# Down weights in three loads of four feature tiles, between transposing loads

## The chip, the cores and the metric

One Trainium2 chip, one of its cores, one launch. The metric is the device time of the kernel in microseconds (us). Five engines work beside each other, each with its own queue of instructions that it works off in order: TensorE (PE in the profile, its weight loads PEld), VectorE (DVE), ScalarE (ACT), GpSimd (POOL) and SyncE (SP), which here does nothing but issue transfers. An engine waits for another one, or for a transfer, at a semaphore.

## The reference

A transformer layer in bfloat16 with S = 2048 tokens and D = 640: linear attention with a softmax feature map (32 heads of 20), then a gated bilinear feed-forward with F = 1536.

```python
def _A_ref(x, wqkv, w_phi, wo):                     # H = 32, Dh = 20
    q, k, v = ...                                   # x @ wqkv, split in heads
    pq = jnp.einsum("bhsd,hdf->bhsf", q, w_phi)
    pk = jnp.einsum("bhsd,hdf->bhsf", k, w_phi)
    phi_q = jnp.concatenate([_softmax(pq, axis=-1), _softmax(-pq, axis=-1)], axis=-1)
    phi_k = jnp.concatenate([_softmax(pk, axis=-1), _softmax(-pk, axis=-1)], axis=-1)
    kv = jnp.einsum("bhsf,bhsd->bhfd", phi_k, v)
    z  = jnp.einsum("bhsf->bhf", phi_k)
    num = jnp.einsum("bhqf,bhfd->bhqd", phi_q, kv)
    den = jnp.einsum("bhqf,bhf->bhq", phi_q, z)[..., None] + 1e-6
    return (num / den, heads joined) @ wo

def _B_ref(x, w_gate, w_up, w_down):
    h = (x @ w_gate) * (x @ w_up)
    return jnp.einsum("bsf,fd->bsd", h, w_down)

h = x + _A_ref(_layernorm(x), A_wqkv, A_w_phi, A_wo)
h2 = h + _B_ref(_layernorm(h), B_w_gate, B_w_up, B_w_down)
```

Only w_down, called Wd in the kernel (1536 x 640, twelve feature tiles of 128 rows), is loaded in another way by the change.

## The kernel before

The tokens are cut into 16 tiles of 128, and four tiles make a block. The program is built as a list of operations (Prog.op, line 195), each with an engine, a function that emits it, and the registers (Reg) that it reads (rd), writes (wr) or adds to (app). From the registers follow the semaphores to wait on. Each operation belongs to a unit with a short name, set by U(...). The order on each engine isn't planned: ORDER (lines 74 to 148) writes it out by hand as a list of unit names, and place (line 244) takes each engine's operations in this order, choosing only which buffer of a pool an operation gets, by modelled times.

The units around the change, for a token tile t:

- kt, Kt, vt: keys, their normalisation and the values. The values go to vaug.
- At: products of keys and values (kv_mm), summed over all tiles; the last readers of vaug as values.
- qt: scores of the queries on TensorE, their maximum on VectorE, exponentials on ScalarE into one of three eq buffers. Qt: sum and reciprocal on VectorE, a product on GpSimd (line 999), and two transposing transfers on SP (line 553) that turn eq into phiqT. The eq buffer is free for another tile when both have landed.
- nt: the attention's numerator on TensorE, from phiqT; quotient into ob on VectorE (line 1075); a transposing transfer on SP that turns ob into oT. For the even block oT lies in the buffer named phik, for the odd block behind Wd in the buffer named vaug. Tiles 0 and 1 are turned by TensorE instead.
- ht: product with Wo on TensorE (phik,Wo or vaug,Wo in the profile), residual, statistics, and the normalised row hb, which SP turns into hT.
- fb.ft.j: gate and up products of block b, feature tile ft.
- T0 to T3: sums of blocks of Wd on GpSimd (weight_sums, line 1247), the first readers of Wd. d0, d1: the down products of tiles 0 and 1 on TensorE (down_raw, line 1279), which read Wd directly.

Wd takes the place of the values in memory: it lies in the buffer BV, named vaug in the profile, and may be written when the last At is done; alias (line 236) hands the readers of vaug on to R_Wd. The unit ld (line 1432) loads it in one transfer of 1920 KB, issued by SP. In SP's order it stands between the two transposes of query tile 4:

`Q5 Q5 n2 n3 Q7 Q7 Q4 ld Q4 Q6 n7 n5 Q6 Q8 Q8`

SP's plain loads (load, line 548) take their semaphores in turn from a ring of eight called w, its transposes from a ring of eight called tr. All of SP's transfers run through one queue of the profile (q1).

Of the kernel before, what the change touches and what calls it, by code (L numbers as in the profile page):

```python
# [11 lines left out]
P = 128  # L12
# [135 lines left out]
}  # L148


# [274 lines left out]
def bass_sequential_preLN__linear_kernel_hedgehog__glu_gated_bilinear__prompt_kernel(  # L425
        nc, A_x, A_wqkv, A_w_phi, A_wo, B_x, B_w_gate, B_w_up, B_w_down, out):
    with ExitStack() as ctx:
        _build(ctx, nc, A_x, A_wqkv, A_w_phi, A_wo, B_w_gate, B_w_up, B_w_down, out)
# [5 lines left out]
def _build(ctx, nc, A_x, A_wqkv, A_w_phi, A_wo, B_w_gate, B_w_up, B_w_down, out):  # L434
    g = Prog(nc, ctx)
# [4 lines left out]
    def regs(n):  # L440
        return [Reg() for _ in range(n)]
# [57 lines left out]
    Wd = BV[:, 0:NF * D].rearrange("p (f n) -> p f n", f=NF)  # L499
# [37 lines left out]
    R_Wo, R_Wgu, R_Wd = regs(NC), regs(2), Reg()  # L537
# [7 lines left out]
    R_phiqT = [[regs(4) for _ in range(2)] for _ in range(2)]  # L545
    R_hT, R_oT, R_hhT = [regs(4) for _ in range(2)], [regs(4) for _ in range(2)], [[regs(4) for _ in range(NF)] for _ in range(2)]

    def load(out_, in_, wr, mb, eng="SP", at=0.0):
        return g.op(eng, lambda e: e.dma_start(out_, in_), wr=wr, dma=("w", 8), t=0.5, lat=0.4 if at else 0.6, size=mb / 0.38, at=at)

    def transpose(out_, in_, rd, wr, use=(), t=1.27, size=0.45, lat=0.3, at=0.0):

# [24 lines left out]
    def U(name):  # L577
        g.unit = name
# [3 lines left out]
    def load_wnat(w, cs=(0, NC), eng="SP", at=0.0):  # L582
        c0, c1 = cs
        load(Wnat[:, c0:c1, :], A_wqkv[P * c0:P * c1, D * w:D * (w + 1)].rearrange("(c p) n -> p c n", p=P), R_Wnat[c0:c1],
             0.3 * (c1 - c0), eng=eng, at=at)
# [4 lines left out]
    def load_x(b):  # L590
        load(x_all[:, 4 * b:4 * b + 4, :], A_x[0, 4 * P * b:4 * P * (b + 1), :].rearrange("(t p) n -> p t n", p=P), [R_x[b]], 0.9)

    def load_wv(c0, c1, at):
        load(Wp[:, c0:c1, 2 * D:3 * D], A_wqkv[P * c0:P * c1, 2 * D:3 * D].rearrange("(c p) n -> p c n", p=P), R_Wp[2][c0:c1], 0.16 * (c1 - c0), at=at)
# [36 lines left out]
    for a in range(NC):  # L631
        lo, hi = CH[a]
        n = hi - lo + 1
# [795 lines left out]
    g.alias([r for a in R_phiqT for b_ in a for r in b_], R_Wnat + R_WT[0] + R_WT[1])  # L1429
    g.alias([r for x in R_hhT for y in x for r in y] + [r for x in R_hT for r in x] + R_oT[0], [r for p in R_phik for r in p])  # L1430
    g.alias(R_oT[1] + [R_Wd], R_vaug)
    U("ld")
    load(Wd[:, :, :], B_w_down.rearrange("(f p) n -> p f n", p=P), [R_Wd], 1.92)
    def each(f, b):
        for t in range(4 * b, 4 * b + 4):
            f(t)
# [82 lines left out]
```

## Time and profile before

| | |
|---|---|
| median of 3 runs | 267.46 us (267.43 to 267.47) |
| profiled execution | 267.44 us |
| its span, first to last instruction | 265.7 us |
| granted TensorE clock | 1.0 throughout |
| bytes moved | 28.65 MB, mean 108 GB/s |
| the down weights' load | issued at 93.54 us, 0.59 us on SP, landed 8.2 us after its issue |

The span is 1.7 us shorter than the time of the same execution; what lies around it is start and end. Times within the profile count from the span's start. In a timeline each line is a merged piece: start, duration, engine (SPq is SP's queue), line of the kernel, operation, written tile<-read tiles, and in brackets idle time and what ended it. A transfer has a duration on SP, which is its issue alone, and a time from issue to landing, which the view of one tile gives as minimum, median and maximum. The view of windows gives for each stretch its busy time on each engine with the number of instructions, then the granted clock, the mean busy share of the 16 DMA engines and the GB/s.

### The profile page before, as it was taken

Reading aid. Unit: us, or ns where it says so; the run is one execution under the profiler, and the core shown is the slowest. Engines: PE = TensorE matmul, PEld = TensorE weight load, DVE = VectorE, ACT = ScalarE, POOL = GpSimd, SP = SyncE. Lnnn points to the kernel's source line nnn. Section 1 sums busy time; section 2 is a strip of 40 time slices with the busy share of each in tenths; the row PEclk is TensorE's granted clock in tenths of the full one; section 3 lists DMA queues with packets and bytes.
Section 4 is the critical chain, followed back from the end, with each engine's and each line's share of the span. In section 5 each row is a group of like instructions: output and inputs, shape, how many; then the busy total and the mean of one; then the engine's idle time right before and its main releaser. Section 6 shows DMA issues by size and latency. Waiting matters only on the chain.

```text
span 265.7 us, 6271 instructions
## 1 busy us (share of the span) xinstructions
PE 261.3 (98%) x2439; PEld 200.2 (75%) x2439; DVE 223.0 (84%) x418; ACT 177.6 (67%) x387; POOL 190.4 (72%) x243
## 2 busy tenths in 40 slices
PE   8999999999999999999999999999999999999995
PEld 8877777776877887777766887777777777777774
DVE  1999999999999876998989788987778788676683
ACT  2567999999857998769562695764856555645221
POOL 5446889999932879999974889359856474648652
PEclk9999999999999999999999999999999999999999
DMA  7996989933255489666866414300420501001012
GB/s 188 305 142 140 170 177 397 390 107 73 40 80 100 93 245 211 130 112 134 119 121 128 46 25 79 99 4 0 52 49 14 88 0 52 1 2 51 4 68 78
DMA packets 67678, 28.65 MB, mean 108 GB/s; under 512 B 57920, under 2 KB 66368, under 8 KB 67648
## 3 DMA queue, kind: packets, MB, share of 16 engines
q1 hardware_dynamic: 66432, 27.77, 47.9%
q10 hardware_dynamic: 1216, 0.48, 0.7%
q8 instruction: 19, 0.31, 0.5%
q14 instruction: 11, 0.09, 0.1%
HBM read 11.82 MB, written 2.62 MB: 54 GB/s over the span
## 4 chain that ended last, share of the span: by engine, by line
PE 80%; POOL 13%; DVE 2%; DMA 2%; issue 1%; ACT 1%; SPq 0%; ACTq 0%
PE ps L657 54%; PE ps L1210 25%; POOL phik L950 10%; DMA phiqT<-eq 2%; POOL eq L999 1%; POOL rs L714 1%; PE ps L746 1%; DVE Wp L864 1%; DVE Ssum L947 1%; ACT eq L933 1%; POOL vaug L645 0%; SPq L553 0%; DVE phiqT L806 0%; DVE ps L925 0%; DVE t L702 0%
## 5 line engine op out<-in xcount | busy, mean ns | idle before, releaser
L657 PE MATMUL ps<-Wp,xT 128*128 128x320 bf16 (+1 forms) x606 | 89.1, 299 | 0.0
L657 PEld LDWEIGHTS ps<-Wp,xT 128*128 128x128 bf16 x606 | 58.0, 98 | 22.6 <-ACT phik L933 0.3
L1240 POOL TENSOR_TENSOR phik<-phik,gate 128x512 bf16<-128x512 bf16 x34 | 40.0, 1182 | 25.9 <-DVE phik L1237 25.5
L1220 ACT ACTIVATE eq<-ps 128x256 f32<-128x256 f32 x110 | 37.4, 386 | 23.0 <-PE ps L1210 18.8
L1210 PE MATMUL ps<-phik,Wgu 128*128 128x256 bf16 (+1 forms) x228 | 50.6, 304 | 0.0
L950 POOL TENSOR_TENSOR phik<-phik,Rk 128x1280 bf16<-128x1280 bf16 x16 | 37.4, 2357 | 5.8 <-DVE Rk L949 4.8
L657 PE MATMUL ps<-phik,Wgu 128*128 128x256 bf16 (+1 forms) x260 | 33.3, 281 | 0.0
L657 PEld LDWEIGHTS ps<-phik,Wgu 128*128 128x128 bf16 x260 | 24.9, 98 | 5.8 <-DMA phik<-hb 0.2
L1337 POOL TENSOR_TENSOR phiqT<-phiqT,x_all 128x320 f32<-128x320 f32 x26 | 21.7, 844 | 9.7 <-ACT phiqT L1335 9.6
L925 DVE TENSOR_REDUCE ps<-ps 128x1 f32<-128x640 f32 (+1 forms) x32 | 26.1, 819 | 2.9 <-PE ps L657 2.9
L1210 PEld LDWEIGHTS ps<-phik,Wgu 128*128 128x128 bf16 x228 | 21.9, 98 | 5.7 <-ACT eq L1220 0.2
L657 PE MATMUL ps<-vaug,phik 128*128 128x63 bf16 (+1 forms) x308 | 25.9, 238 | 0.0
L987 DVE TENSOR_REDUCE Sq<-eq 128x66 f32<-128x1320 bf16 x16 | 24.2, 1514 | 1.2 <-ACT eq L933 1.2
L1237 DVE TENSOR_TENSOR phik<-ps,eq 128x512 bf16<-128x512 f32 x28 | 19.2, 687 | 6.3 <-PE ps L1210 6.2
L1335 ACT ACTIVATE phiqT<-ps 128x320 f32<-128x320 f32 x26 | 11.4, 437 | 19.3 <-PE ps L657 19.2
L947 DVE TENSOR_REDUCE Ssum<-phik 128x64 f32<-128x1280 bf16 x16 | 23.4, 1462 | 0.0
L1235 DVE TENSOR_TENSOR gate<-ps,eq 128x512 bf16<-128x512 f32 x27 | 18.5, 686 | 5.2 <-PE ps L1210 2.9
L657 PEld LDWEIGHTS ps<-vaug,phik 128*128 128x128 bf16 x308 | 18.1, 97 | 5.3
L999 POOL TENSOR_TENSOR eq<-eq,rq 128x660 bf16<-128x660 bf16 x16 | 20.9, 1306 | 0.8
L933 ACT ACTIVATE eq<-ps,nb,rs 128x300 bf16<-128x300 f32 (+2 forms) x26 | 17.2, 690 | 6.0 <-DVE nb L928 4.2
L1342 DVE TENSOR_TENSOR outb<-ps,phiqT 128x320 bf16<-128x320 f32 x27 | 12.9, 488 | 6.6 <-PE ps L657 5.1
L1139 ACT ACTIVATE gate<-ps 128x256 bf16<-128x256 f32 (+1 forms) x26 | 10.4, 403 | 10.2 <-PE ps L657 9.6
(169 smaller groups left out, 527.4 us busy)
## 6 DMA issues: line engine op xcount, KB each, us to landing
x_all<-in_A_x_dram SPq DMA_DIRECT2D x4, 640.0 KB, 10.8
out_dram<-outb SPq DMA_DIRECT2D x13, 160.0 KB, 1.8
Wgu<-in_B_w_gate_dram SPq DMA_DIRECT2D x1, 1920.0 KB, 11.1
Wgu<-in_B_w_up_dram SPq DMA_DIRECT2D x1, 1920.0 KB, 16.6
vaug<-in_B_w_down_dram SPq DMA_DIRECT2D x1, 1920.0 KB, 8.2
Wp<-in_A_wqkv_dram SPq DMA_DIRECT2D x1, 800.0 KB, 5.1
phiqT<-in_A_wqkv_dram SPq DMA_DIRECT2D x1, 800.0 KB, 6.3
Wo<-in_A_wo_dram SPq DMA_DIRECT2D x1, 800.0 KB, 6.3
```

The costliest lines, as they stand in the source:

```text
L657: ins = e.matmul(o_, lhsT=l_, rhs=r_, start=s_, stop=p_, skip_group_check=True)
L925: g.op("DVE", lambda e: e.tensor_reduce(out=mx(), in_=src(), axis=AX.XY if len(src().shape) == 3 else AX.X, op=ALU.max, apply_absolute_val ...
L933: g.op("ACT", lambda e, s=s, sc=sc, to=to, of=of: e.activation(out=to(s), in_=of(), func=ACT.Exp, bias=nb[:, i:i + 1], scale=sc[:, t:t + 1 ...
L947: g.op("DVE", lambda e: e.tensor_reduce(out=Ssum[:, vs.i, :], in_=x, axis=AX.X, op=ALU.add), rd=R_phik[t], wr=vs.R, use=[vs], t=1.39, lat=1.5)
L950: g.op("POOL", lambda e: e.tensor_tensor(out=x, in0=x, in1=Rk[:, vr.i, :].unsqueeze(2).to_broadcast([P, 2 * H, DH]), op=ALU.mult), rd=vr.R ...
L987: g.op("DVE", lambda e: e.tensor_reduce(out=Sq[:, vs.i, :].rearrange("p (w g) -> p w g", w=NQ), in_=feat(0, NQ).rearrange("p w (g f) -> p ...
L999: return e.tensor_tensor(out=x, in0=x, in1=rq[:, vr.i, :].rearrange("p (w h) -> p w h", h=HW).unsqueeze(3).to_broadcast([P, NQ, HW, DH]), ...
L1210: ins = e.matmul(o_, lhsT=l_[0](c), rhs=m_, start=fr, stop=False, skip_group_check=True)
L1220: g.op("ACT", lambda e: e.activation(out=half(s[i], 256 * h, 256 * (h + 1)), in_=PS[v.i][:, bk, 256:512], func=ACT.Copy), rd=[v.R[bk]], wr ...
L1237: g.op("DVE", lambda e: e.tensor_tensor(out=hhT[:, hb_, ft, :], in0=PS[v.i][:, 1, :], in1=half(s[1]), op=ALU.add), rd=[v.R[1]] + s[1].R, w ...
L1240: g.op(eng, lambda e: e.tensor_tensor(out=hhT[:, hb_, ft, :], in0=hhT[:, hb_, ft, :], in1=gate[:, vg.i, :], op=ALU.mult), rd=R_out + vg.R, ...
L1337: g.op("POOL", lambda e: e.tensor_tensor(out=slot(x), in0=slot(x), in1=x_all[:, t, c], op=ALU.add), rd=x.R + [R_h[t]], wr=x.R, use=[x], t= ...
```

## The change

The load of Wd is cut into three, one for each four feature tiles (640 KB each), as units ld0, ld1 and ld2. The first writes R_Wd, the other two add to it (app), so that each reader of Wd waits for all three. In SP's order ld0 goes between Q5 and n2, ld1 between n3 and Q7, ld2 between Q7 and Q4. The two transposes of Q4 are now neighbours. Everything else in the orders of all engines is kept.

```diff
     "SP":
-        "Q0 Q1 Q0 Q1 Q2 Q2 Q3 Q3 Q5 Q5 n2 n3 Q7 Q7 Q4 ld Q4 Q6 n7 n5 Q6 Q8 Q8 h3 n4 h2 Q10 Q10 n6 Q14 Q14 Q9 n8 Q9 h5 h7 Q11 Q11 "
...
+        "Q0 Q1 Q0 Q1 Q2 Q2 Q3 Q3 Q5 Q5 ld0 n2 n3 ld1 Q7 Q7 ld2 Q4 Q4 Q6 n7 n5 Q6 Q8 Q8 h3 n4 h2 Q10 Q10 n6 Q14 Q14 Q9 n8 Q9 h5 h7 "
...
-    def load(out_, in_, wr, mb, eng="SP", at=0.0):
-        return g.op(eng, lambda e: e.dma_start(out_, in_), wr=wr, dma=("w", 8), t=0.5, lat=0.4 if at else 0.6, size=mb / 0.38, at=at)
+    def load(out_, in_, wr, mb, eng="SP", at=0.0, first=True):
+        return g.op(eng, lambda e: e.dma_start(out_, in_), **{"wr" if first else "app": wr}, dma=("w", 8), t=0.5, lat=0.4 if at else 0.6, size=mb / 0.38, at=at)
...
-    U("ld")
-    load(Wd[:, :, :], B_w_down.rearrange("(f p) n -> p f n", p=P), [R_Wd], 1.92)
+    for j in range(3):
+        U("ld%d" % j)
+        load(Wd[:, 4 * j:4 * j + 4, :], B_w_down[4 * P * j:4 * P * (j + 1), :].rearrange("(f p) n -> p f n", p=P), [R_Wd], 0.64,
+             first=j == 0)
```

4 rows, old and new, of the table ORDER are left out of this document.

## The prediction

> **What bounds the kernel now.** I read the page first (busy shares, chain that ended last), then the chain in order of time, then the timelines of SP's queue and of TensorE around the edited place.
>
> ```profile
> span 265.7 us, 6271 instructions
> PE 261.3 (98%) x2439; PEld 200.2 (75%) x2439; DVE 223.0 (84%) x418; ACT 177.6 (67%) x387; POOL 190.4 (72%) x243
> PE 80%; POOL 13%; DVE 2%; DMA 2%; issue 1%; ACT 1%; SPq 0%; ACTq 0%
> ```
>
> ```profile
> 84.20 51.29 PE ps L657 x487
> 135.50 12.44 PE ps L657 x102
> ```
>
> The first fence says that TensorE is nearly always busy; the second (chain of waits: start, duration, what) says that from 84.20 us on the chain is TensorE alone, 51.29 us in one piece and then on to the end. All edits lie in this stretch. So time lost by TensorE here is lost for good, and time can be won only where TensorE waits here. TensorE's queue is fixed, so one late operand stops everything behind it.
>
> ```profile
> 82.02 2.53 SPq L553 DMA_TRANSPOSE phiqT<-eq  x2
> 84.60 2.93 SPq L553 DMA_TRANSPOSE phik<-ob  x2
> 88.32 5.17 SPq L553 DMA_TRANSPOSE phiqT<-eq  x3
> 93.54 0.59 SPq L549 DMA_DIRECT2D vaug<-in_B_w_down_dram  x1
> 94.17 5.46 SPq L553 DMA_TRANSPOSE phiqT<-eq  x2
> ```
>
> In SP's timeline (start, duration of the merged piece, queue, line) these are Q5 Q5, then n2 n3, then Q7 Q7 and the first Q4, then the load ld, then the second Q4 and the first Q6. Each consumer of these transposes is in TensorE's weight loads:
>
> ```profile
> 85.65 3.25 PEld L657 LDWEIGHTS ps<-phik,Wgu 128*128 128x128 bf16 x30
> 88.91 2.68 PEld L657 LDWEIGHTS ps<-Wo,phik 128*128 128x128 bf16 x20
> 91.63 2.74 PEld L657 LDWEIGHTS ps<-phik,Wgu 128*128 128x128 bf16 x25
> 94.39 0.48 PEld L657 LDWEIGHTS ps<-Phi,phiqT 128*128 128x128 bf16 x11
> 105.06 0.39 PEld L657 LDWEIGHTS ps<-Phi,phiqT 128*128 128x128 bf16 x11 [0.17 <-ACT eq L933]
> 113.18 0.44 PEld L657 LDWEIGHTS ps<-phik,Wgu 128*128 128x128 bf16 x5 [0.25 <-DMA phik<-hb]
> 135.49 0.39 PEld L657 LDWEIGHTS ps<-Phi,phiqT 128*128 128x128 bf16 x11 [0.33 <-DVE phik L1148]
> ```
>
> At 88.91 the twenty weight loads of h2 and h3 start without a wait. At 94.39 n7 starts, which reads Q7's transposes. The last three rows are the only ones between 82 and 140 us in which the weight loads idled for something besides 81.76, which is ahead of the edit: 0.17, 0.25 and 0.33 us.
>
> **What can be won.** These idle times are upper bounds, since weight loads run ahead of the matmuls. For the second, the matmul rows (start, merged duration, shape, count) show the rest:
>
> ```profile
> 109.85 3.42 PE L657 MATMUL ps<-vaug,phik 128*128 128x320 bf16 x24
> 113.19 0.72 PE L657 MATMUL ps<-phik,Wgu 128*128 128x256 bf16 x5
> 125.35 3.42 PE L657 MATMUL ps<-vaug,phik 128*128 128x320 bf16 x24
> 128.61 0.50 PE L657 MATMUL ps<-Phi,phiqT 128*128 128x63 bf16 x11
> ```
>
> The same 24 matmuls take 113.19 - 109.85 = 3.34 us before the wait and 128.61 - 125.35 = 3.26 us without one, so that wait costs 0.08 us, a third of its 0.25. By the same third the first costs 0.06 us. Both hang on SP being late: the first on ScalarE's exponentials of tile 10, which need the eq buffer that the second Q4 frees, the second on the transpose of h2, and the load is what made SP late:
>
> ```profile
> L553 SPq DMA_TRANSPOSE phiqT<-eq x1: 3227/3227/3227, 94.2 to 94.2; - x1
> DMA to landing us min/median/max: 8.3/8.3/8.3
> ```
>
> This is the second Q4, issued behind the whole load: it holds SP for 3.23 us and lands 8.3 us after its issue, at 102.5. In the new order Q4 stands behind one third only, and SP catches up. I count both waits as gone: -0.14 us. The third (0.33) is ended by VectorE 22 us later and I leave it. If all three went by their upper bounds the gain would be 0.75 us; that is the most that this stretch can give.
>
> **The moved loads.** The edit adds two DMA issues of 0.59 us each on SP (row at 93.54). ld1 stands between n3 and Q7, where SP is free: 84.60 + 2.93 = 87.53 to 88.32; ld2 between Q7 and Q4, whose issue SP would wait for anyway (the last of the three in 5.17 us, against about 1.25 for an undisturbed one). Those two issues cost nothing; without such gaps they would cost 0.6 us each of SP, which is not the bound. ld0 is different: it takes SP at 82.02 + 2.53 = 84.55 us, when n2 is ready:
>
> ```profile
> 82.92 0.82 DVE L1075 TENSOR_TENSOR ob<-ps,rden 128x640 bf16<-128x640 f32 x1
> L553 SPq DMA_TRANSPOSE phik<-ob x1: 1276/1276/1276, 84.6 to 84.6; - x1
> DMA to landing us min/median/max: 2.6/2.6/2.6
> ```
>
> ob of tile 2 is done at 83.74, and its transpose, issued at 84.60, lands 2.6 us later, at 87.2: 1.7 us ahead of h2's first weight load at 88.91. That 1.7 us is all the cover ld0 has. ld0 itself waits for nothing: the readers of vaug (kv_mm) are ahead of n2's matmuls in TensorE's order. What does it do to n2? Issue: +0.6 us. Then the queue: how 640 KB issued on SP ahead of a transpose behave is shown by the first x_all load, of the same size and row length:
>
> ```profile
> L549 SPq DMA_DIRECT2D x_all<-in_A_x_dram x1: 580/580/580, 22.8 to 22.8; - x1
> DMA to landing us min/median/max: 5.4/5.4/5.4
> L553 SPq DMA_TRANSPOSE xT<-in_A_x_dram x1: 1225/1225/1225, 23.5 to 23.5; - x1
> DMA to landing us min/median/max: 5.5/5.5/5.5
> L549 SPq DMA_DIRECT2D x_all<-in_A_x_dram x1: 580/580/580, 35.6 to 35.6; - x1
> DMA to landing us min/median/max: 4.6/4.6/4.6
> ```
>
> The load issued at 22.83 lands at 28.2, the transpose behind it at 28.9, 0.7 later. ld and the second Q4 say the same: 93.54 + 8.2 = 101.7 (page) and 102.5, again 0.7 later. So on this queue a transpose lands after the load ahead of it, never past it.
>
> ```profile
> vaug<-in_B_w_down_dram SPq DMA_DIRECT2D x1, 1920.0 KB, 8.2
> 94.50:95.50 1.00, 1.00 (x20) 0.83 (x18) 0.47 (x2) 1.00 (x4) 0.97 (x3) 1.00 0.49 35
> 95.50:96.50 1.00, 1.00 (x12) 0.90 (x10) 0.79 (x2) 1.00 (x3) 0.92 (x3) 1.00 0.82 233
> 96.50:97.50 1.00, 1.00 (x12) 0.90 (x10) 0.57 (x1) 1.00 (x4) 0.92 (x2) 1.00 1.06 392
> ```
>
> And the windows (last column GB/s) show why a third of a load is more than a third of 8.2 us: it starts slowly. From 94.5 to 97.5 it moves 35 + 233 + 392 = 660 KB, so the first third (655 KB) is through 4.0 us after its issue; the steady rate alone would take 1.7.
>
> The sum: ld0 issued at 84.56, landing 4.6 us later (the x_all load at 35.6, the one nearest to the 4.0 us in which the bytes of a third were through) at 89.2; n2 lands 0.7 later, at 89.9; h2, due at 88.91, starts at 89.9: **+1.0 us**. Lower end: it lands with its last byte, 4.0 + 0.7 gives 89.25, +0.35. Upper end: 5.4 + 0.7 gives 90.65, +1.75. n3, issued about 1.3 us behind n2, follows within about 0.7 us and is due 1.36 us after h2 (half of 91.63 - 88.91), so it is covered. With the two waits gone, 1.0 - 0.14 = **+0.86 us**. The reading of Wd is no issue: the earliest reader starts at 102.92 and all three thirds should be in by about 98.
>
> ```profile
> 102.92 1.39 POOL L1261 TENSOR_TENSOR Wp<-vaug 128x640 bf16<-128x640 bf16 x1
> ```
>
> That reader and d1 wait on three semaphores instead of one: below 0.1 us on an engine that has slack.
>
> The profiled execution took 267.44 us, against a median of 267.46, so 267.44 + 0.86 = 268.3.
>
> The Trainium skill, "DMA: Bandwidth & Descriptors", section "Anatomy of one DMA — SWDGE (gpsimd) path", fits a DMA as 2.0 us plus its bytes at 436 GB/s, measured on another issuing path; by it, as an estimate, a third would land after 3.5 us. The trace disagrees: 4.6 and 5.4 us for that size. And "Perfetto Trace Analysis", section "DMA Optimizations", says that splitting DMAs can let some start sooner; here the start is not what is short, since no reader waits for Wd.
>
> **The rivals.**
>
> A, not slower: ld0 hides in n2's cover. If the slow start is a matter of the moment at 94.5 and not of the load (other traffic fell there too), a third costs about 0.95 us to its first packet (93.54 to 94.5), 655 KB at 392 GB/s = 1.7 us, and 4.6 - 4.0 = 0.6 us to land: 84.56 + 3.25 = 87.8, n2 at 88.5, before 88.91. It decides at a landing of 3.65 us for ld0. Then only the gain is left: 267.44 - 0.14 = 267.3, at most 266.7 if all three waits go. Against it: three loads that started on a quiet queue (22.8, 35.6, 93.54) needed 4.0 us or more for 655 KB. By the fit of the Trainium skill above, an estimate, ld0 would also come out on this side. Chance 0.25, and beside it 0.06 for the larger gain.
>
> B, a second stall: Q7 stands behind ld1, and n7 needs it.
>
> ```profile
> L553 SPq DMA_TRANSPOSE phiqT<-eq x1: 1292/1292/1292, 89.6 to 89.6; - x1
> DMA to landing us min/median/max: 4.5/4.5/4.5
> 94.17 0.60 ACT L933 ACTIVATE eq<-ps,nb,rs 128x300 bf16<-128x300 f32 x1
> ```
>
> Its second half lands at 89.6 + 4.5 = 94.1, only 0.3 us ahead of n7 (94.39) and just before ScalarE's exponentials of tile 8 (94.17), which reuse the buffer. Behind ld0, n2, n3 and a slow-starting ld1 it could land at 95 to 96. TensorE and ScalarE come 1.0 us later themselves, to 95.4 and 95.2, so it decides at about 95.2; the price is up to 0.8 us more: 269.1. For it: the pile of three loads in one queue; against it: a load queued behind others need not pay a slow start, and without it ld1 takes 1.7 us and Q7 lands near 94.5. Chance 0.17.
>
> That the edit does nothing is excluded: SP's order is written out, and the loads' old semaphore holders landed tens of microseconds earlier.
>
> **How the numbers follow.** Forecast 268.3, chance 0.52, its own range 267.6 to 269.1 (+0.35 - 0.14 to +1.75 - 0.14). About 0.2% (0.53 us) can be told from no change here. The forecast's lower edge, 0.08 of its 0.52, falls within that. Slower: 0.44 + 0.17 = 0.61. Same: 0.25 + 0.08 = 0.33. Faster: 0.06. The range runs from A's 267.3, less a little, to B's 269.1 plus its spread: 267.2 to 269.4 leaves out the larger gain and a part of B.
>
> **What would show it.** In the changed kernel: h2's weight loads idle for 0.7 to 1.7 us, ended by DMA phik<-ob; a first vaug load that takes 4.5 to 5.4 us to land; a second Q4 that lands within about 5 us rather than 8.3; no DMA wait of ScalarE near 102.5; the waits at 105 and 113 gone. No idle time at h2 makes A right; idle time at n7 or ahead of tile 8's exponentials makes B right. The forecast is wrong in its reason if the time is lost after 100 us, where I have SP better off than before.

## The result and the profile after

| | before | after |
|---|---|---|
| median, 4 runs each on one chip | 267.44 us (267.18 to 267.47) | 269.58 us (269.16 to 269.69) |
| profiled execution | 267.44 us | 269.16 us |
| its span | 265.7 us | 267.4 us |

The change is slower: ratio 1.0076, 95% interval 1.0063 to 1.0089, 2.1 us by the medians. It lies just above the range of the prediction. The profiled execution of after is the fastest of its four, so its trace accounts for 1.7 us; the other three took 0.4 to 0.5 us more and left no trace.

The page of after, its span and busy times:

```profile
span 267.4 us, 6259 instructions
PE 260.5 (97%) x2424; PEld 200.3 (75%) x2439; DVE 222.7 (83%) x418; ACT 177.8 (66%) x387; POOL 190.4 (71%) x243
```

The engines do the same work in the same order (the small difference in counts is matmul records missing from the trace); TensorE is busy for a smaller share of a longer span. So it waits. Where, the chain of waits of after says (start, duration, what), which before was TensorE alone from 84.20 on:

```profile
85.13 4.91 DMA phik<-ob
90.08 5.64 PE ps L657 x45
95.73 0.65 issue
96.37 0.51 PE ps L657 x11
96.88 0.36 ACT gate L1139
97.24 0.28 ACT phik L1143
97.57 41.48 PE ps L657 x396
```

One transfer, the transpose n2, is now on the chain for 4.91 us, and around 96 to 97.5 TensorE waits again, partly for ScalarE. From 97.57 to 224 us TensorE is alone on it, but for gaps of 0.05 us. TensorE's weight loads in the timeline of after name the same two places:

```profile
85.37 3.25 PEld L657 LDWEIGHTS ps<-phik,Wgu 128*128 128x128 bf16 x30
90.08 2.58 PEld L657 LDWEIGHTS ps<-Wo,phik 128*128 128x128 bf16 x20 [1.47 <-DMA phik<-ob]
96.34 0.40 PEld L657 LDWEIGHTS ps<-Phi,phiqT 128*128 128x128 bf16 x11 [0.90 <-issue]
97.57 3.17 PEld L657 LDWEIGHTS ps<-phik,Wgu 128*128 128x128 bf16 x30 [0.43 <-ACT phik L1143]
107.10 0.48 PEld L657 LDWEIGHTS ps<-Phi,phiqT 128*128 128x128 bf16 x11
115.11 0.56 PEld L657 LDWEIGHTS ps<-phik,Wgu 128*128 128x128 bf16 x5
```

The first bracket is h2 waiting for n2 (1.47 us). The second is n7: the view says "issue" because it finds no releaser, but n7 reads Q7's transposes, the second of which lands at 96.3, as shown below. The third follows from it: ScalarE's exponentials of tile 8 were waiting for the same transpose, so the next feed-forward copy came late. 1.47 + 0.90 + 0.43 = 2.80 us. The last two rows are the places that idled before for 0.17 and 0.25 us; they have no bracket now, and the 0.33 us at 135.5 has none either: 2.80 - 0.75 = 2.05. TensorE had also reached h2 0.3 us earlier in this execution (85.37 + 3.25 = 88.62, against 88.91), for reasons ahead of the edit, and 2.05 - 0.3 is about the 1.7 us of the span. The brackets are upper bounds on both sides: held against the same rows of before, TensorE's weight loads go from 0.28 us early (85.37 against 85.65) to 2.20 us late (101.63 against 99.43), so the three waits are worth 2.48 us, and 0.41 us of it come back by 137.79 (136.00 in before).

SP's timeline of after shows why n2 and Q7 are late:

```profile
84.50 0.58 SPq L549 DMA_DIRECT2D vaug<-in_B_w_down_dram  x1
85.13 2.59 SPq L553 DMA_TRANSPOSE phik<-ob  x2
87.76 0.58 SPq L549 DMA_DIRECT2D vaug<-in_B_w_down_dram  x1
88.39 2.67 SPq L553 DMA_TRANSPOSE phiqT<-eq  x2
91.11 0.58 SPq L549 DMA_DIRECT2D vaug<-in_B_w_down_dram  x1
```

and the views of single transfers of after (issue, then time to landing) give what followed, for ld0, n2 and the second Q7:

```profile
L549 SPq DMA_DIRECT2D vaug<-in_B_w_down_dram x1: 582/582/582, 84.5 to 84.5; - x1
DMA to landing us min/median/max: 4.9/4.9/4.9
L553 SPq DMA_TRANSPOSE phik<-ob x1: 1199/1199/1199, 85.1 to 85.1; - x1
DMA to landing us min/median/max: 4.9/4.9/4.9
L553 SPq DMA_TRANSPOSE phiqT<-eq x1: 1404/1404/1404, 89.7 to 89.7; - x1
  ACT eq L933: 1.2, 1
DMA to landing us min/median/max: 6.6/6.6/6.6
```

SP begins each of these issues within 0.1 us of the end of the one ahead of it. The time is lost behind the issue: ld0 lands at 89.4, n2 at 90.0 (before: 87.2), the second Q7 at 96.3 (before: 94.1), and ScalarE waited 1.2 us for the last.

### The profile page after: what moved, and what is told of

Same layout as the page of the kernel before. It is cut to its first block, busy times and chain, and to the rows that moved or that the text cites. A ratio compares the mean times of both kernels' runs of the same rounds, so it can differ in the third digit from the quotient of the medians.

```text
span 267.4 us, 6259 instructions
## 1 busy us (share of the span) xinstructions
PE 260.5 (97%) x2424; PEld 200.3 (75%) x2439; DVE 222.7 (83%) x418; ACT 177.8 (66%) x387; POOL 190.4 (71%) x243
## 4 chain that ended last, share of the span: by engine, by line
PE 90%; DVE 4%; DMA 2%; issue 1%; ACT 1%
PE ps L657 66%; PE ps L1210 24%; DMA phik<-ob 2%; DVE ob L1075 1%; PE ps L746 1%; DVE x_all L1093 1%; DVE ps L925 1%; DVE Sq L987 1%; ACT phiqT L1335 0%; ACT eq L1220 0%; DVE phiqT L806 0%; DVE rden L1073 0%; DVE rq L993 0%; DVE Phi L1037 0%; ACT gate L1139 0%
## 5 line engine op out<-in xcount | busy, mean ns | idle before, releaser
L657 PE MATMUL ps<-Wp,xT 128*128 128x320 bf16 (+1 forms) x606 | 89.1, 299 | 0.0
L1210 PE MATMUL ps<-phik,Wgu 128*128 128x256 bf16 (+1 forms) x214 | 46.6, 299 | 0.2
L657 PE MATMUL ps<-phik,Wgu 128*128 128x256 bf16 (+1 forms) x259 | 33.4, 280 | 0.2 <-ACT phik L1143 0.2
```

The costliest lines, as they stand in the source:

```text
L657: ins = e.matmul(o_, lhsT=l_, rhs=r_, start=s_, stop=p_, skip_group_check=True)
L1210: ins = e.matmul(o_, lhsT=l_[0](c), rhs=m_, start=fr, stop=False, skip_group_check=True)
```

## The experiments

The theory: a transpose issued behind a load lands after it. What a load costs is decided by the reader of the transposes behind it, at two places here: n2 behind ld0 (reader h2) and Q7 behind ld1 (readers n7 and ScalarE). The rivals: the cutting itself costs (three slow starts, three semaphores), SP's time for issues costs, or n7's stall is only an after-effect of the first.

All medians, with the ratio to the kernel before on the same chip:

| kernel | us | ratio | 95% interval |
|---|---|---|---|
| the change | 269.58 | 1.0076 | 1.0063 to 1.0089 |
| three loads at the old place | 267.17 | 0.9994 | 0.9984 to 1.0004 |
| only ld0 early | 268.37 | 1.0040 | 1.0028 to 1.0052 |
| only ld0 early, again | 268.34 | 1.0034 | 1.0022 to 1.0045 |
| only ld1 early | 268.79 | 1.0048 | 1.0033 to 1.0062 |
| only ld2 early | 267.26 | 0.9994 | 0.9967 to 1.0020 |
| the change, ld1 behind Q7 | 268.60 | 1.0046 | 1.0028 to 1.0065 |
| 160 KB ahead of n2 | 267.10 | 0.9987 | 0.9962 to 1.0011 |
| 320 KB ahead of n2 | 267.36 | 0.9990 | 0.9964 to 1.0015 |
| 160 KB ahead of Q7 | 267.32 | 1.0012 | 0.9988 to 1.0036 |
| all behind Q4 | 269.77 | 1.0090 | 1.0065 to 1.0115 |
| only ld0 early, from ScalarE | 268.00 | 1.0019 | 1.0007 to 1.0031 |
| all three from ScalarE | 274.09 | 1.0249 | 1.0209 to 1.0288 |

### The parts one by one

The cut without the move:

```diff
-Q5 Q5 ld0 n2 n3 ld1 Q7 Q7 ld2 Q4 Q4 Q6
+Q5 Q5 n2 n3 Q7 Q7 Q4 ld0 ld1 ld2 Q4 Q6
```

> Three loads, all three at the old place of the one load (between the two transposes of tile 4). Theory (the queue is worked off in order, so what counts is which transpose stands behind a load, and how long its consumer can wait): no stall at h2 and none at n7, 267.2 to 267.7 us. Rival 1 (it is the cutting itself: two more loads, each with its slow start, and three semaphores to wait on): about as slow as the change, 269 us or more. Rival 2 (the stalls come from the issue time on SP): 267.4 to 268.

267.17 us, the time of before. Cutting the load costs nothing, so the change's loss is all in where the pieces stand.

The first part alone:

```diff
-Q5 Q5 ld0 n2 n3 ld1 Q7 Q7 ld2 Q4 Q4 Q6
+Q5 Q5 ld0 n2 n3 Q7 Q7 Q4 ld1 ld2 Q4 Q6
```

> ld0 alone ahead of n2, ld1 and ld2 at the old place of the one load. Theory: h2 stalls by 1.2 to 1.5 us as in the changed kernel, n7 does not; 268.4 to 268.8 us. Rival 1 (cutting): 269 us or more. If the loss at n7 in the changed kernel needed only the late n2 and n3 and not ld1, n7 stalls here too and the time is near 269.5.

268.37 us, and once more on another occasion:

> ld0 alone early on SP once more, on the same chip as the run with ld0 on ScalarE: 268.2 to 268.9 us, h2 stalls by 1.2 to 1.4 us in all.

268.34 us. TensorE's weight loads of the first of these runs idle at h2 and a little at h3, and not at n7:

```profile
90.09 1.21 PEld L657 LDWEIGHTS ps<-Wo,phik 128*128 128x128 bf16 x10 [1.29 <-DMA phik<-ob]
91.61 1.21 PEld L657 LDWEIGHTS ps<-Wo,phik 128*128 128x128 bf16 x10 [0.30 <-DMA phik<-ob]
```

So ld0 is worth about 1.0 us, and n7's stall doesn't follow from a late n2 and n3.

The second part alone:

```diff
-Q5 Q5 ld0 n2 n3 ld1 Q7 Q7 ld2 Q4 Q4 Q6
+Q5 Q5 n2 n3 ld1 Q7 Q7 Q4 ld0 ld2 Q4 Q6
```

> ld1 alone early, between n3 and Q7; ld0 and ld2 at the old place of the one load. Theory: no stall at h2; Q7 lands behind ld1 at about 95 to 96 instead of 94.1, n7 and ScalarE's exponentials of tile 8 wait for it, 0.8 to 1.6 us; 268.0 to 268.9 us. Rival (the second stall comes only from the pile of ld0, n2, n3 and ld1): below 0.4 us, 267.3 to 267.8.

268.79 us, 1.3 us by the ratio. The weight loads of this run, and its second Q7:

```profile
95.48 0.40 PEld L657 LDWEIGHTS ps<-Phi,phiqT 128*128 128x128 bf16 x11 [1.10 <-issue]
96.71 3.17 PEld L657 LDWEIGHTS ps<-phik,Wgu 128*128 128x128 bf16 x30 [0.44 <-ACT phik L1143]
```

```profile
L553 SPq DMA_TRANSPOSE phiqT<-eq x1: 1343/1343/1343, 89.7 to 89.7; - x1
DMA to landing us min/median/max: 5.8/5.8/5.8
```

No stall at h2; n7 and then the feed-forward copy stall as in the change. No pile of earlier transfers is needed: ld1 alone delays Q7 enough.

The third part alone:

```diff
-Q5 Q5 ld0 n2 n3 ld1 Q7 Q7 ld2 Q4 Q4 Q6
+Q5 Q5 n2 n3 Q7 Q7 ld2 Q4 ld0 ld1 Q4 Q6
```

> ld2 alone early, between Q7 and the first Q4; ld0 and ld1 at the old place of the one load. Theory: Q4 lands up to 2 us later than before, but its reader n4 comes only at 105; no stall, 267.0 to 267.6 us. Rival (each early load costs): 268 or more. With the other two parts this should add up to the change: 0 + the first alone + the second alone + this.

267.26 us: nothing. Q4 is late too (its first half lands at 96.5), but nobody reads it before 105. Each of these runs holds the cut as well, so a part's own factor is its ratio over that of the cut alone: 1.0046 (1.0040 / 0.9994), 1.0054 and 1.0000. With the cut's 0.9994 they multiply to 1.0094, against the change's 1.0076 (up to 1.0089 by its interval): the parts account for all of it. The little that they have more is within the intervals of the parts; it may also come from TensorE and ScalarE, which in the change come to n7 late already and wait there for less (1.33 us of idle weight loads in after, 1.54 with ld1 alone).

And the change with ld1 put behind Q7:

```diff
-Q5 Q5 ld0 n2 n3 ld1 Q7 Q7 ld2 Q4 Q4 Q6
+Q5 Q5 ld0 n2 n3 Q7 Q7 ld1 ld2 Q4 Q4 Q6
```

> The change with one part undone: ld1 behind Q7 instead of ahead of it (ld0 n2 n3 Q7 Q7 ld1 ld2 Q4 Q4). Theory: the stall at h2 stays (1.2 to 1.4 us), the one at n7 goes; 268.1 to 268.7 us, as with ld0 alone early. Rival (n7's stall is a consequence of the late n2 and n3): about 269.5, as the change.

268.60 us. In its timeline of weight loads the stall at h2 stays, and n7 has none:

```profile
90.11 2.58 PEld L657 LDWEIGHTS ps<-Wo,phik 128*128 128x128 bf16 x20 [1.39 <-DMA phik<-ob]
```

### How many bytes may stand there

Wd cut into one feature tile (or two) and the rest, the first piece ahead of n2, the rest at the old place:

```diff
-    for j in range(3):
+    for j, (f0, f1) in enumerate(((0, 1), (1, 12))):      # or ((0, 2), (2, 12))
         U("ld%d" % j)
-        load(Wd[:, 4 * j:4 * j + 4, :], B_w_down[4 * P * j:4 * P * (j + 1), :].rearrange("(f p) n -> p f n", p=P), [R_Wd], 0.64,
+        load(Wd[:, f0:f1, :], B_w_down[P * f0:P * f1, :].rearrange("(f p) n -> p f n", p=P), [R_Wd], 0.16 * (f1 - f0),
              first=j == 0)
```

> One feature tile of Wd (160 KB) ahead of n2, the other eleven in one load at the old place. If a load starts slowly (35 KB in its first microsecond, as in the profile of before): it lands 3.0 to 3.5 us after its issue, n2 about 0.6 us later at 88.1 to 88.6, just within h2's cover; no stall or below 0.2 us, 267.2 to 267.6 us. If only bytes count (392 GB/s): it lands after about 2.0 us and n2 at 87.3, no stall, same time. The landing tells the two apart. If the stall at h2 came from the issue on SP and not from the transfer, h2 stalls here by more than 1 us too, 268.4.

> Two feature tiles (320 KB) ahead of n2, the other ten in one load at the old place. With the slow start: the load lands 3.6 to 3.9 us after its issue, n2 at 88.8 to 89.1, h2 stalls by 0.1 to 0.5 us, 267.3 to 267.8 us. By bytes alone: lands after 2.4 us, n2 at 87.7, no stall, 267.2 to 267.4.

267.10 and 267.36 us: no loss that can be told. The issue on SP is the same 0.58 us as in the change, so it isn't what costs. The landing of the first piece, with one tile and with two:

```profile
L549 SPq DMA_DIRECT2D vaug<-in_B_w_down_dram x1: 580/580/580, 84.6 to 84.6; - x1
DMA to landing us min/median/max: 2.8/2.8/2.8
```

```profile
L549 SPq DMA_DIRECT2D vaug<-in_B_w_down_dram x1: 582/582/582, 84.9 to 84.9; - x1
DMA to landing us min/median/max: 3.6/3.6/3.6
```

2.8, 3.6 and (four tiles, above) 4.9 us for 164, 328 and 655 KB: a little over 2.0 us and then 0.7 to 0.8 us for each 164 KB. For 160 KB that is between the two expectations, sooner than the slow start would have it and later than bytes alone at 392 GB/s; for 320 KB, 3.6 us, it is at the lower edge of the slow start's. With 320 KB n2 lands at 89.1, at the very edge of h2's cover; with 640 KB it is past it.

The same dose at the other place, 160 KB ahead of Q7:

```diff
-Q5 Q5 ld0 n2 n3 ld1 Q7 Q7 ld2 Q4 Q4 Q6
+Q5 Q5 n2 n3 ld0 Q7 Q7 Q4 ld1 Q4 Q6
```

> One feature tile (160 KB) between n3 and Q7, the other eleven in one load at the old place: the place of ld1 with a quarter of its bytes. If the stall at n7 comes from the bytes ahead of Q7: Q7's second half lands at 94.1 to 94.8, n7 stalls by at most 0.5 us, 267.1 to 267.9 us. If any load there costs the whole stall (because it meets a pause of the transfers that falls there anyway): n7 and ScalarE lose more than 1 us, 268.4 or more.

267.32 us. Its second Q7, to be held against the 5.8 us above and the 4.5 us of before:

```profile
L553 SPq DMA_TRANSPOSE phiqT<-eq x1: 1288/1288/1288, 89.9 to 89.9; - x1
DMA to landing us min/median/max: 4.5/4.5/4.5
```

It is as early as without any load there. So it is the number of bytes ahead of Q7 that costs, not the place as such.

### A later place

```diff
-Q5 Q5 ld0 n2 n3 ld1 Q7 Q7 ld2 Q4 Q4 Q6 n7 n5 Q6
+Q5 Q5 n2 n3 Q7 Q7 Q4 Q4 ld0 ld1 Q6 ld2 n7 n5 Q6
```

> A place meant to be better than both kernels': both Q4 together, then ld0 and ld1, Q6, ld2, n7, n5. Every transpose behind a load has a reader that comes late. Theory: no stall from a load, the waits at 105 and 113 us gone, 266.9 to 267.3 us. Rival (the loads collide with n7 and n5, which are read from 106 on): 267.5 to 268.5.

269.77 us: the expectation was wrong, and its rival explains only a small part of the loss. The timelines of GpSimd, ScalarE and TensorE in this run:

```profile
104.99 1.40 POOL L1261 TENSOR_TENSOR Wp<-vaug 128x640 bf16<-128x640 bf16 x1 [1.98 <-DMA vaug<-in_B_w_down_dram]
```

```profile
107.43 0.38 ACT L1139 ACTIVATE gate<-ps 128x256 bf16<-128x256 f32 x1 [2.34 <-POOL phik L1145]
```

```profile
108.23 2.90 PE L657 MATMUL ps<-Wo,vaug 128*128 128x320 bf16 x20 [1.32 <-ACT phik L1143]
```

In this order: the first sum of Wd on GpSimd, due at 102.9, waits 1.98 us for ld2; GpSimd's feed-forward products stand behind it in its queue, ScalarE waits 2.34 us for these, and TensorE's matmuls idle for 1.32 us (its weight loads for 1.62) until ScalarE's copy. The transfer that ended this wait was the load itself. The rival's collision was there too, but ended sooner: n7's transpose, issued behind ld2, landed at 107.0, 0.4 us after the weight loads at 108.20 were due. So Wd has a due time too, and between "ahead of transposes that are read soon" and "after 102.9" there are few places; the old one is among them. No version was found that beats before beyond the interval. Behind the edit's place the TensorE of before idled for 0.75 us at most, so there was little to find.

### Another queue

The loads issued by ScalarE, whose transfers go through a queue of their own (q10 in the page), all three:

```diff
-             first=j == 0)
+             eng="ACT", first=j == 0)
...
 "ACT":
-h0 h1 f0.4.0 h0 f0.4.0 f0.10.0 f0.10.0 f0.0.0 q6
+h0 h1 ld0 f0.4.0 h0 f0.4.0 f0.10.0 ld1 f0.10.0 f0.0.0 ld2 q6
 "SP":
-Q5 Q5 ld0 n2 n3 ld1 Q7 Q7 ld2 Q4 Q4 Q6
+Q5 Q5 n2 n3 Q7 Q7 Q4 Q4 Q6
```

> The three loads at about the same moments as in the change (85.3, 87.9 and 89.7 us), but issued by ScalarE, so that they stand in another DMA queue than the transposes. Theory (a transpose waits for the load ahead of it in the same queue): n2 lands at most 0.5 to 1 us later than before instead of 2.8, no stall or a short one at h2, 267.2 to 268.0 us; ScalarE pays three issues of 0.5 us in its idle time. Rival (it is the DMA engines' work, in whatever queue, that delays the transposes): h2 stalls by about 1.3 us as before, 269 us or more.

274.09 us, far worse than any other. The theory as stated there, that only the queue's own order matters, fell: n2 lands 5.4 us after its issue, though SP's queue held transposes alone. The loads went out at 84.1, 87.5 and 88.9 us (in the change at 84.5, 87.8 and 91.1, not at the moments that the expectation gives), so that ld2, too, was ahead of the second Q7 (89.5), which in the change it is not. The second Q7 and what followed, in this run's view of the transfer, the weight loads and the windows (the figure before the last two is the granted clock):

```profile
L553 SPq DMA_TRANSPOSE phiqT<-eq x1: 1730/1730/1730, 89.5 to 89.5; - x1
DMA to landing us min/median/max: 9.5/9.5/9.5
```

```profile
99.09 0.40 PEld L657 LDWEIGHTS ps<-Phi,phiqT 128*128 128x128 bf16 x11 [3.31 <-issue]
```

```profile
100.30:103.70 3.40, 3.38 (x16) 2.40 (x17) 2.40 (x3) 2.85 (x8) 2.95 (x5) 0.50 0.00 0
104.00:106.00 2.00, 2.00 (x28) 1.82 (x27) 0.21 (x1) 1.85 (x6) 1.92 (x5) 1.00 0.70 140
```

Q7 behind all three loads lands after 9.5 us, n7 idles for 3.31 us, and then TensorE works at half clock from 100.3 to 103.7. To separate the queue from the order, ld0 alone early, from ScalarE, the others on SP at the old place:

```diff
-             first=j == 0)
+             eng="ACT" if j == 0 else "SP", first=j == 0)
...
 "ACT":
-h0 h1 f0.4.0 h0
+h0 h1 ld0 f0.4.0 h0
 "SP":
-Q5 Q5 ld0 n2 n3 ld1 Q7 Q7 ld2 Q4 Q4 Q6
+Q5 Q5 n2 n3 Q7 Q7 Q4 ld1 ld2 Q4 Q6
```

> ld0 alone early, issued by ScalarE (at about 84.1 us, in the other DMA queue, 0.4 us ahead of n2's issue on SP); ld1 and ld2 on SP at the old place. If the order of issue counts whatever the queue: n2 lands 0.6 us behind ld0, h2 stalls by 0.9 to 1.3 us, as with ld0 on SP, 268.1 to 268.8 us. If a queue of its own lets the transposes pass: no stall, 267.1 to 267.5. If two queues at once cost more than their bytes: over 269.

268.00 us, beside 268.34 for the same with ld0 on SP, on the same chip. The transpose n2 of this run, issued behind it on SP, and the weight loads:

```profile
L553 SPq DMA_TRANSPOSE phik<-ob x1: 1284/1284/1284, 85.3 to 85.3; - x1
DMA to landing us min/median/max: 4.8/4.8/4.8
```

```profile
90.11 1.21 PEld L657 LDWEIGHTS ps<-Wo,phik 128*128 128x128 bf16 x10 [0.69 <-DMA phik<-ob]
91.97 1.21 PEld L657 LDWEIGHTS ps<-Wo,phik 128*128 128x128 bf16 x10 [0.65 <-DMA phik<-ob]
```

The transposes don't pass the load on another queue: n2 lands 4.8 us after its issue. Its first stall is shorter than with ld0 on SP because TensorE came to h2 later in this execution, the slowest of its ten (at 89.4, against 88.8 there). The Trainium skill, "DMA: Bandwidth & Descriptors", section "Issuing engines are not separate DMA queues", says that transfers run on the same 16 engines and interleave, whoever issues them; the trace agrees in that the other queue gave n2 no way past the load. The 0.3 us between the medians of the two runs may come from SP's free 0.58 us; that wasn't tried by itself.

## Why the prediction was wrong

**The bound** was right: TensorE alone sets the end after 84 us, and what it idles is what the time grows by (2.05 us of idle time added, less 0.3).

**n2 behind ld0** was right in mechanism and nearly in size: ld0 was to land after 4.6 us and n2 at 89.9; they landed after 4.9 us and at 90.0. The stall is 1.47 us of idle weight loads instead of 1.0, because TensorE came 0.3 us earlier to h2 than in the execution of before, which isn't part of the loss. Alone, with the gains in it, it makes the kernel 0.34 to 0.40% slower, 0.9 to 1.1 us, where the sum was 0.86.

**The gains** were right: the waits at 105 and 113 us are gone, worth 0.15 us by the rows of TensorE (the sum has 0.14), and with three loads at the old place they are still there (0.16 and 0.21 us of idle weight loads). The wait at 135.5 us, gone in after, is gone in that run too, so the move isn't what removed it. Nor did the issues of ld1 and ld2, or the third load, cost anything.

**The step that failed** is the wait of n7 and ScalarE for Q7 behind ld1, which the sum puts at nothing. The reason is under rival B: "a load queued behind others need not pay a slow start, and without it ld1 takes 1.7 us and Q7 lands near 94.5". The first part of this held, the second didn't. ld1 landed at 93.4, 2.6 us behind n3 (90.8), where ld0 had needed 4.9 us from its issue. This is the first of Q7's two transposes (issue, then time to landing):

```profile
L553 SPq DMA_TRANSPOSE phiqT<-eq x1: 1227/1227/1227, 88.4 to 88.4; - x1
DMA to landing us min/median/max: 5.7/5.7/5.7
```

It landed at 94.1, 0.7 us behind ld1, as the prediction has it for a transpose behind a load, and the second at 96.3, 2.2 us later and past the 95.2 at which B was to decide. The prediction doesn't say how it came to 94.5. Its own terms are n3 at 90.6, 1.7 us for ld1 and 0.7 us to Q7's first transpose; with the 2.3 us that lie between the landings of Q7's two transposes in before (91.8 and 94.1) they give 95.3, which is at the limit already. The rest is ld1, which took 2.6 us instead of 1.7. So n7's weight loads idled for 0.90 us and those behind ScalarE's copy for 0.43 us, where the sum has nothing. The signs that the prediction gave for its forecast and for B both came: idle time at h2, a first load of 4.9 us, and idle time at n7 and ahead of tile 8's exponentials. The windows of after around ld1 and Q7, whose last column is GB/s, counted where packets start:

```profile
90.00:91.00 1.00, 0.92 (x7) 0.68 (x8) 0.00 (x0) 1.00 (x4) 0.92 (x2) 1.00 1.09 320
91.00:92.00 1.00, 1.00 (x9) 0.70 (x8) 0.33 (x2) 0.64 (x2) 1.00 (x2) 1.00 1.04 356
92.00:93.00 1.00, 1.00 (x10) 0.73 (x8) 0.56 (x1) 0.41 (x1) 0.27 (x1) 1.00 1.57 121
93.00:94.00 1.00, 1.00 (x11) 0.90 (x10) 0.96 (x3) 0.93 (x4) 0.19 (x1) 1.00 1.05 225
94.00:95.00 1.00, 1.00 (x11) 0.90 (x10) 1.00 (x1) 1.00 (x3) 0.00 (x0) 1.00 1.63 35
```

From 90 to 92 the transfers run at 320 and 356 GB/s, near the 392 of a long load. Then the traffic breaks down twice, at 92 to 93 and at 94 to 95, while Q7's transposes are still to be done, and the second Q7 lands at 96.3. Such a hole was in the trace of before as well:

```profile
92.00:93.00 1.00, 1.00 (x12) 0.90 (x10) 1.00 (x3) 1.00 (x4) 0.56 (x2) 1.00 0.09 22
```

The prediction read Q7's landing, 4.5 us after its issue against n2's 2.6, without asking what the other 1.9 us were. In hindsight, with only 0.3 us of lead and a hole in the transfers just there, 640 KB ahead of Q7 were the likelier loss, not the one in six that they were given. The prediction's B was also too cheap: up to 0.8 us, against 1.33 us of idle weight loads in after (0.90 + 0.43; by the rows of before and after 1.13) and 1.54 with ld1 alone (1.10 + 0.44). It has one wait, from 95.2 to 96 at most; there are two, one after the other, since ScalarE's exponentials wait for the same transpose and hand on a second wait. With B's price at what ld1 alone costs, 1.3 us, the sum is 267.44 + 0.86 + 1.3 = 269.6, the measured median. That it fits to the tenth is luck: the parts measured one by one multiply to 1.0094, which is 270.0.

What makes the holes is open. In these traces a 16 KB packet of the instruction queue (q8 in the page) begins at 92.1 in before and at 93.6 in after, within the hole or just ahead of it. In every trace here such a packet begins within 0.6 us of the landing of Q7's first transpose, and the second lands 2.1 to 2.5 us after the first (3.1 with all three loads from ScalarE). So ld1 may have delayed Q7's second transpose by its own bytes or by way of that packet; no run moved the packet by itself.

## What to carry to other kernels

A load placed ahead of small transfers can hold all of them up until it has landed, so count the lead of each one's reader over its landing, not the load's own due time alone, and give the load to a stretch where the smallest lead is larger than the delay, and which is over before the load's own reader is due. Cutting the load cost nothing here, and gained nothing: ahead of n2 and of Q7, with leads of 1.7 and 0.3 us, 160 KB cost nothing and 640 KB cost time. Where a transfer takes longer than its like in the trace of before, find out what it waited for before building on its lead.

## What the runs showed of the hardware that was not expected

A load on another DMA queue delays the transposes that are issued after it as one on the same queue does: n2 took 4.8 us behind a load from ScalarE, 4.9 behind one from SP and 2.6 without. In the trace of ld0 alone from ScalarE even the second transpose of Q5, issued on SP 0.8 us ahead of the load, landed 5.4 us after its issue, against 2.8 in the others; why is not shown.

TensorE's clock was granted at 0.50 from 100.3 to 103.7 us in the one trace in which its weight loads had idled for 3.3 us, and at 1.0 after the idle times of 0.9 to 1.5 us in the change and with ld0 or ld1 alone. The Trainium skill, "TensorE: Matmul & The Clock Gate", section "What's actually happening", has the array at half rate after an idle window of about 3.4 us and back after a busy one as long; the trace nearly agrees, with a slightly shorter idle time (3.3 us of weight loads, 3.1 of matmuls) ahead of 3.4 us at half clock. The clock adds a step to the price of a wait: in that run 3.4 us at half clock are 1.7 us of work lost on top of the idle time.

A load ahead of n2 took a little over 2.0 us and then 0.7 to 0.8 us for each 164 KB up to 655 KB, a little over half of the rate that a long load reaches (392 GB/s in one window of before). The 164 KB ahead of Q7 took 2.5 us, against 2.8 ahead of n2.
